# Loading both plain x tiles ahead of the first K row, and taking the last output columns as 512, 288 and 224

## The chip, the cores and the metric

The kernel runs on 1 core of one Trainium2 chip. The metric is the device time of one execution in microseconds; the profile gives a span that is some 1.5 us shorter. "Dense stream" below means the 30 matmuls of 512 columns that run back to back once the first weights are there.

## The reference, cut to what matters

```python
x = A_x                                             # 1 x 2048 x 1024, bf16
g = sigmoid((x * gate_w).sum(-1, keepdims=True))
a = linear_attention(x, wqkv, wo)                   # 32 heads of 32, phi(q), phi(k)
b = x + scatter_of_one_row(ffn(x[argmax(x @ w_r)])) # one routed token
return g * a + (1 - g) * b
```

The kernel first needs K and V for all tokens: x transposed, against the K and V columns of `wqkv`. It ends with one matrix product per 128 tokens against a merged matrix of attention state and `wo`, plus the mix with x.

## The kernel before: the parts concerned

The front. Two x tiles are loaded as they are and transposed on TensorE, the other tiles come by transposing fetches. The weights for K come as eight pieces of 256 KB, called K row 0 to 7 here.

```python
load_x(0, 1)
load_k(0)
load_x(1, 1)
for c in range(1, KC):
    load_k(c)
# ... V columns, transposing fetches, the rest of V, the Q weights
...
warm(N_WARM)                       # 6 matmuls of 512 columns on constants
...
unit_T(0)                          # 8 transposes, evicted by VectorE and ScalarE
warm(3, 128)
first_mm(0, 0, 1)                  # tile 0 x K row 0: 2 matmuls of 512
wps = ps_ffn.tile([P, 16], BF, tag="f")
pe.transpose(wps[:], wrg_rows[:], ident[0:16, 0:16])   # router and gate weights
dve.tensor_copy(wkv[:, :, 2 * D : 2 * D + 2], ...)
unit_T(1)
for c in range(1, KC):             # the dense stream
    first_mm(0, c, c + 1)
    if c < KC - 1:
        first_mm(1, c - 1, c)
```

The back, for the last of 16 token tiles: each group of columns is eight matmuls, one VectorE instruction from PSUM to SBUF, and its own store.

```python
cols = [(0, 512), (512, 512)] if t < NT - 1 else [(0, 512), (512, 384), (896, 128)]
for c0, cw in cols:
    ps = ps_work.tile([P, 512], F32, tag="w")
    for g in range(NG):
        pe.matmul(ps[:, 0:cw], lhsT=pq_all[...], rhs=m_sb[:, g, c0 : c0 + cw], ...)
    dve.scalar_tensor_tensor(ot[:, c0 : c0 + cw], ps[:, 0:cw], gate[:, t : t + 1], xg[...], ...)
    if t == NT - 1:
        nc.sync.dma_start(out=out2d[...], in_=ot[:, c0 : c0 + cw])
```

## Time and profile before

| | before |
|---|---|
| median of the first 3 runs | 248.74 us (248.62 to 249.12) |
| TensorE busy | 97% of the span |
| dense stream begins | 6.54 us, 0.04 after K row 1 lands |
| from the start of the first short column group to the last landing | 4.11 us |

The profile is of a run of 248.56 us. The prediction shows the page and the timelines. One more view is of use, the busy time of each engine by stretch (bounds, length, then busy time and number of instructions of each engine, granted clock, DMA share, GB/s), here of the kernel before:

```profile
0.00:3.00 3.00, 1.98 (x5) 0.73 (x6) 0.00 (x0) 1.10 (x1) 2.02 (x27) 1.00 0.32 80
3.00:6.50 3.50, 3.50 (x24) 1.88 (x23) 0.65 (x3) 0.77 (x2) 1.93 (x13) 1.00 0.99 334
```

From 3.0 to 6.5 us TensorE (first figure after the length) is shown busy in all 3.50 us, while the loads run at a DMA share of 0.99. Both look like the bound, and a busy TensorE does not say which: the warm-up matmuls on constants and the slow clock fill time that nobody needs. The clock column says nothing of that slow clock: its record begins when the full clock opens, at 6.09 us here, and the time before is shown as 1.00. The two rates are read from the steps of the 512-column matmuls, 0.427 us before and 0.216 after.

### The profile page before, as it was taken

To read this page: it belongs to the slowest core of one execution; us is meant where nothing else is said; L and a number is where in the kernel's file an instruction comes from. 1 tells how busy PE (TensorE), PEld (TensorE's weight loads), DVE (VectorE), ACT (ScalarE), POOL (GpSimd) and SP (SyncE) were. 2 spreads that over 40 slices of the span, in tenths; PEclk is the share of its full clock that TensorE was granted. 3 is DMA by queue.
4 is the path that set the end of the run, shared out by engine and by line. 5 is a ranking of instruction groups with operands and counts; after the bars stand their busy time and mean duration, and the time that the engine had idled before them with its cause. 6 is when DMAs were issued, how large, how long until landed. Compare 5 with 4: busy or idle time off the path is not lost.

```text
span 247.0 us, 4867 instructions
## 1 busy us (share of the span) xinstructions
PE 240.8 (97%) x1898; PEld 123.6 (50%) x1923; DVE 172.7 (70%) x264; ACT 127.6 (52%) x215; POOL 52.5 (21%) x100
## 2 busy tenths in 40 slices
PE   8999999999999999999999999999999999999994
PEld 3466756654554554554554555544443444444442
DVE  0053124379984989845989999996789999954342
ACT  3195343355566376545555555668887633333300
POOL 6000000400000100000003300101666689950000
PEclk9999999999999999999999999999999999999999
DMA  6999995499969993599699690000004754464122
GB/s 207 343 239 195 267 392 151 108 326 337 281 194 292 341 290 88 149 312 384 224 345 340 230 280 3 3 4 21 0 3 127 204 182 148 155 190 166 48 82 86
DMA packets 46311, 47.78 MB, mean 193 GB/s; under 512 B 16776, under 2 KB 35472, under 8 KB 46224
## 3 DMA queue, kind: packets, MB, share of 16 engines
q1 hardware_dynamic: 45648, 46.28, 61.5%
q0 software_dynamic: 608, 1.19, 1.7%
q8 instruction: 15, 0.25, 0.5%
q14 instruction: 8, 0.07, 0.1%
q10 hardware_dynamic: 32, 0.00, 0.0%
HBM read 39.33 MB, written 8.39 MB: 193 GB/s over the span
## 4 chain that ended last, share of the span: by engine, by line
PE 97%; issue 1%; DVE 0%; DVEq 0%
PE ps L83 88%; PE first L83 3%; PE kvacc L83 2%; PE warm_ps L83 1%; PE red L83 1%; PE dps L83 1%; PE pst L83 1%; PE pm L83 1%; DVE ot L83 0%; PE yps L83 0%; PE pt L83 0%; DVEq L739 0%; PE hps L83 0%; PE rps L83 0%; PE wps L83 0%
## 5 line engine op out<-in xcount | busy, mean ns | idle before, releaser
L83 PE MATMUL ps<-wkv,xT 128*128 128x352 bf16 (+2 forms) x600 | 106.1, 334 | 0.4
L83 PEld LDWEIGHTS <-xT 128*128 128x128 bf16 x640 | 62.1, 98 | 49.1 <-issue 0.3
L83 ACT ACTIVATE u<-ps 128x512 f32<-128x512 f32 x60 | 35.9, 598 | 46.3 <-PE ps L83 45.7
L83 PE MATMUL ps<-xT,wq 128*128 128x512 bf16 x245 | 57.3, 379 | 0.6 <-issue 0.2
L83 PE MATMUL ps<-m_sb,pq_all 128*128 128x512 bf16 (+2 forms) x259 | 55.4, 373 | 0.3
L83 ACT ACTIVATE e<-u 128x512 f32<-128x512 f32 x64 | 40.3, 630 | 2.0
L83 PEld LDWEIGHTS <-pq_all 128*128 128x128 bf16 x264 | 25.4, 98 | 30.2 <-issue 0.7
L641 POOL TENSOR_TENSOR pq_all<-pq_all,rb 128x512 bf16<-128x512 bf16 x32 | 36.4, 1171 | 12.1 <-DVE rb L83 11.5
L83 PEld LDWEIGHTS <-wq 128*128 128x128 bf16 x256 | 24.5, 98 | 28.2 <-issue 1.0
L83 DVE SCALAR_TENSOR_TENSOR gacc<-wt,hcol,gacc 128x1024 f32<-128x1024 bf16 x27 | 34.5, 1278 | 0.4
L83 DVE SCALAR_TENSOR_TENSOR ot<-ps,gate,xg 128x512 bf16<-128x512 f32 (+2 forms) x33 | 23.9, 738 | 14.3 <-PE ps L83 13.1
L83 DVE SCALAR_TENSOR_TENSOR gacc<-wt,xs_f,gacc 128x2048 f32<-128x2048 bf16 x14 | 32.8, 2345 | 0.2
L83 ACT ACTIVATE xg<-xt,omg 128x1024 f32<-128x1024 bf16 x16 | 18.2, 1147 | 26.8 <-DVE ot L83 25.8
L83 DVE SCALAR_TENSOR_TENSOR pq_all<-ps,e 128x512 bf16<-128x512 f32 x32 | 21.9, 687 | 11.3 <-ACT e L83 11.3
L83 DVE SCALAR_TENSOR_TENSOR pk<-ps,e 128x512 bf16<-128x512 f32 x28 | 19.0, 686 | 11.8 <-ACT e L83 11.6
L83 DVE STREAM_SHUFFLE rb<-rdp 128x512 f32<-128x512 f32 x32 | 22.8, 753 | 0.0
L83 ACT CAST vt<-ps 128x352 bf16<-128x352 f32 x32 | 14.4, 453 | 11.4 <-PE ps L83 11.1
L214 POOL MEMSET vt<- 128x22 bf16 x16 | 3.7, 432 | 75.7 <-PE kvacc L83 75.2
L83 ACT CAST vc<-ps 128x320 bf16<-128x320 f32 x16 | 6.5, 428 | 7.3 <-PE ps L83 7.3
L83 DVE COPY rg<-ps 128x2 f32<-128x2 f32 x16 | 2.5, 159 | 10.2 <-ACT vc L83 10.1
L355 POOL DMA_DIRECT2D xs<-in_A_x_dram x1 | 0.7, 711 | 39.3 <-DVE sig L83 39.3
L83 DVE SCALAR_TENSOR_TENSOR pk<-first,e 128x512 bf16<-128x512 f32 x4 | 2.8, 692 | 7.9 <-ACT e L83 7.9
(100 smaller groups left out, 94.9 us busy)
## 6 DMA issues: line engine op xcount, KB each, us to landing
wt<-in_B_w_down_dram SPq DMA_DIRECT2D x14, 512.0 KB, 4.9
wt<-in_B_w_gate_dram SPq DMA_DIRECT2D x8, 512.0 KB, 7.6
wt<-in_B_w_up_dram SPq DMA_DIRECT2D x8, 512.0 KB, 8.3
xt<-xp SPq DMA_DIRECT2D x16, 256.0 KB, 2.7
out_dram<-ot SPq DMA_DIRECT2D x15, 256.0 KB, 2.0
wt<-in_B_w_gate_dram SPq DMA_DIRECT2D x8, 384.0 KB, 7.6
wt<-in_B_w_up_dram SPq DMA_DIRECT2D x8, 384.0 KB, 7.2
wkv<-in_A_wqkv_dram SPq DMA_DIRECT2D x8, 256.0 KB, 4.4
```

What stands on the lines that cost most here:

```text
L83: inst = fn(*a, **k)
L214: nc.gpsimd.memset(vt_t[t][:, :, 32:33], 1.0)
L355: nc.gpsimd.dma_start(out=xs8[:], in_=x2d[bass.ds(idx_val, 1), :].rearrange("o (c p) -> (o c) p", p=P))
L641: nc.gpsimd.tensor_tensor(sl, sl, rb[:], op=ALU.mult)
```

## The change

Its intent: have the transposes of both tiles over before any K row is needed, so that these and the router transpose no longer stand between K row 0 and the dense stream; and balance the last two column groups, so that the last store isn't held up. The router transpose also takes its PSUM buffer from the pool of the tile transposes (`ps_t`, three buffers) in place of `ps_ffn`.

```diff
     load_x(0, 1)
-    load_k(0)
     load_x(1, 1)
-    for c in range(1, KC):
+    for c in range(KC):
         load_k(c)
...
     unit_T(0)
-    warm(3, 128)
-    first_mm(0, 0, 1)
-    wps = ps_ffn.tile([P, 16], BF, tag="f")
+    wps = ps_t.tile([P, 16], BF, tag="t")
     pe.transpose(wps[:], wrg_rows[:], ident[0:16, 0:16])
     dve.tensor_copy(wkv[:, :, 2 * D : 2 * D + 2], ...)
+    warm(2, 128)
     unit_T(1)
+    warm(4, 128)
+    first_mm(0, 0, 1)
...
-        cols = ... else [(0, 512), (512, 384), (896, 128)]
+        cols = ... else [(0, 512), (512, 288), (800, 224)]
```

More of the change, by code (lines that the diff above doesn't have):

```diff
@@ L696 @@
         ot = fin.tile([P, D], BF, tag="o3")
-        cols = [(0, 512), (512, 512)] if t < NT - 1 else [(0, 512), (512, 384), (896, 128)]
+        cols = [(0, 512), (512, 512)] if t < NT - 1 else [(0, 512), (512, 288), (800, 224)]
         for c0, cw in cols:
```

## The prediction

> **What bounds the kernel now.** I read the page first (busy shares, slices, chain of waits), then the timeline of TensorE over the first 26 us, then the landings of the loads that stand there, then the timeline of the last 5 us. The page:
>
> ```profile
> span 247.0 us, 4867 instructions
> PE 240.8 (97%) x1898; PEld 123.6 (50%) x1923; DVE 172.7 (70%) x264; ACT 127.6 (52%) x215; POOL 52.5 (21%) x100
> ...
> PE   8999999999999999999999999999999999999994
> ...
> PE 97%; issue 1%; DVE 0%; DVEq 0%
> ```
>
> TensorE is busy in all slices but the first and the last, and it is 97% of the chain that ended last. Matmul busy time includes pipeline drain, so I do not take it as distance from the peak. What matters is that there is no large hole: only the two ends, about 6.5 us at the front and 4 us at the back, can be changed by this diff, since it touches nothing between.
>
> The front, TensorE alone (start, length, name, idle time before in brackets):
>
> ```profile
> 1.02 2.72 PE L83 MATMUL warm_ps<-const-bfloat16-1.0 128*128 128x512 bf16 x6 [1.02 <-PEq L728]
> 3.72 1.03 PE L83 MATMUL pst<-ident,xnat 128*128 128x128 bf16 x8
> 4.55 0.53 PE L83 MATMUL warm_ps<-const-bfloat16-1.0 128*128 128x128 bf16 x3
> 4.87 1.06 PE L83 MATMUL first<-wkv,xT 128*128 128x512 bf16 x2
> 5.86 0.19 PE L83 MATMUL wps<-ident,wrg_rows 16*128 16x16 bf16 x1
> 5.98 0.65 PE L83 MATMUL pst<-ident,xnat 128*128 128x128 bf16 x8
> 6.54 6.63 PE L83 MATMUL first<-wkv,xT 128*128 128x512 bf16 x29
> 13.01 13.18 PE L83 MATMUL ps<-wkv,xT 128*128 128x322 bf16 x85
> ```
>
> The eight transposes of x tile 0 at 3.72 step by (4.55 - 3.72)/8 = 0.104 us, the eight of tile 1 at 5.98 by (6.54 - 5.98)/8 = 0.07 us, the last of them by about 0.055. From 6.54 to 13.01 there are 30 matmuls (one of 32 is missing from the records, two ran before): 0.216 us each, without a hole. The clock record says full speed from 6.1 us.
>
> The loads that stand there. First the plain x tiles (0 and 1), then K row 0 and K row 1 alone, then the V columns:
>
> ```profile
> DMA to landing us min/median/max: 2.7/3.2/3.8
> ```
> ```profile
> DMA to landing us min/median/max: 2.8/2.8/2.8
> ```
> ```profile
> DMA to landing us min/median/max: 4.1/4.1/4.1
> ```
> ```profile
> wkv<-in_A_wqkv_dram SPq DMA_DIRECT2D x1, 640.0 KB, 7.2
> ```
>
> x tile 0 is issued at 0.98 and lands at 3.7; K row 0 at 1.44, lands 4.3; x tile 1 at 1.90, lands 5.7; K row 1 at 2.39, lands 6.5. So the dense stream begins at 6.54 because K row 1 is there at 6.5; TensorE was itself done with the transposes at about 6.48. The V columns, issued at 5.71, land at 12.9, and their first matmul is at 13.01. A third gate stands at 20.68, where the first tile of the next group of x comes in by a transposing fetch:
>
> ```profile
> 20.68 5.31 PEld L83 LDWEIGHTS <-xT 128*128 128x128 bf16 x39 [0.18 <-DMA xT<-in_A_x_dram]
> ```
>
> The weight load came 0.18 us later than it could have, while the matmul behind it lost nothing. So at 6.5, 13.0 and 20.7 us TensorE and the loads arrive together, within 0.1 us. The front is as much bound by loads as by TensorE.
>
> The back (eviction of the 384 columns, of the 128 columns, the two stores):
>
> ```profile
> 242.94 0.62 DVE L83 SCALAR_TENSOR_TENSOR ot<-ps,gate,xg 128x384 bf16<-128x384 f32 x1 [0.49 <-PE ps L83]
> ```
> ```profile
> 243.47 0.34 DVE L83 SCALAR_TENSOR_TENSOR ot<-ps,gate,xg 128x128 bf16<-128x128 f32 x1
> ```
> ```profile
> 243.58 0.33 SPq L706 DMA_DIRECT2D out_dram<-ot  x1
> ```
> ```profile
> 244.01 0.38 SPq L706 DMA_DIRECT2D out_dram<-ot  x1
> ```
> ```profile
> out_dram<-ot SPq DMA_DIRECT2D x1, 128.0 KB, 1.7
> out_dram<-ot SPq DMA_DIRECT2D x1, 96.0 KB, 1.6
> out_dram<-ot SPq DMA_DIRECT2D x1, 32.0 KB, 1.5
> ```
>
> The last matmul ends at 243.35. The 128-column eviction ends at 243.81, but its store is issued only at 244.01: the store of the 384 columns holds the issuing engine from 243.58 to 243.92. The last store lands at 244.01 + 1.5 = 245.5, and the remaining 1.5 us to 247.0 is a closing sequence of semaphores that the change doesn't touch.
>
> **What the Trainium skill says.** "TensorE: Matmul & The Clock Gate", Part 1, says that the array runs at half rate until an activity window of about 3.4 us was busy, and that the window is free-running, so the moment varies from run to run. The trace agrees on the rates: about 0.107 us for 128 columns early, 0.216 us for 512 after 6.1. Part 4 of the same page says that transposes do not count as busy in the same way; nothing in this trace shows or denies it. "DMA: Bandwidth & Descriptors", Specifications, wants at least 512 B a piece for full rate, with read-modify-write below. At this size no penalty is seen: the store with 256 B rows took 1.5 us, that with 768 B rows 1.6. The same page, Anatomy of one DMA, puts a fixed cost of about 2 us on a transfer, mostly the receipt; here the fixed part is about 1.5, and it can't be split away.
>
> **The change part by part.**
>
> 1. The swap of loads. x tile 1 takes the second place, K row 0 the third; both are 256 KB with 2 KB pieces. I expect x tile 1 at about 4.3 (4.3 to 4.9) and K row 0 at about 5.7. K row 1 stays fourth, with the same bytes ahead, so it lands at 6.5 as before. The order of all later loads is unchanged, so their gates at 13.0 and 20.7 stay.
>
> 2. The order on TensorE. Before: 8 transposes, 3 short warm-up matmuls, 2 matmuls of K row 0 at the slow clock, the router weights' transpose, 8 transposes, 30 matmuls. After: 8 transposes, router transpose, 2 short ones, 8 transposes, 4 short ones, 2 matmuls of K row 0, 30 matmuls. Working forward from 4.55: the 16-row router transpose costs a change of shape on either side (before, it came 0.56 us after a matmul of 0.43, so 0.14 extra, and held the next one for 0.12): 4.55 + 0.14 + 0.12 = 4.81. Two short ones at 0.107: 5.02. x tile 1 is there. Eight transposes at 0.107: 5.88. In the built program their two PSUM banks are those of tile 0's first half and of the router transpose, both emptied by VectorE, the first at 4.79, so I see no wait of weight. Four short ones, two slow, and two fast once the clock opens at 6.1: about 6.2. Two matmuls of K row 0 at the full clock, 0.43: 6.63. Against 6.54 that is +0.09 us. What it wins is that these two no longer run at the slow clock (2 x 0.21 us); what it pays is 3 more short matmuls (0.2 to 0.3) and the transposes of tile 1, which now run wholly at half rate (0.86 against 0.56). If the clock opens earlier, TensorE waits for K row 1 at 6.5 and the front costs 0. So +0.05, between 0 and +0.1. It can hardly be a gain: K row 1, V columns and the transposing fetch hold it within 0.05 us of where it is.
>
> 3. The last columns. Eight matmuls of 384 and eight of 128 took 8 x 0.1625 + 8 x 0.0557 = 1.745 us. With the slope of these two, 288 costs 0.1224 and 224 costs 0.0957, and the sum is 1.745 again: the last matmul ends at the same 243.35. The 288-column eviction begins about 0.32 us before the old one and lasts about 0.51 (0.34 + 160 x 1.07 ns, from 384 in 0.62 and 128 in 0.34): it ends at about 243.14, and its store is issued from 243.16 to 243.50, out of the way. The 224-column eviction begins at about 243.39 (0.04 after the last matmul, as the 384 one did) and lasts 0.44: 243.83. Its store goes at once, 243.86 in place of 244.01, and lands in about 1.57 us (between 1.54 for 256 B and 1.63 for 768 B rows): 245.43 in place of 245.54. Gain 0.11 us.
>
> Sum: 248.74 + 0.05 - 0.11 = 248.68; I say 248.65.
>
> **The rivals.**
>
> Clock gate opens later. The short matmuls and the two of K row 0 kept the array busy before; in the new order the stretch from 3.7 to 5.9 is nearly all transposes. If these count little, the window that ended at 6.1 holds only about 1.4 us of counted work in place of about 2.0, the clock might stay low for one window more, to 9.5, and half of the 14 matmuls of that stretch would be lost: 3.0 us at half rate is 1.5 us lost, about 250.2. Against it: the author put six short matmuls around the transposes, and from 1.0 us there is nearly no idle time. I give it 0.15.
>
> The new order frees TensorE. If K row 1 came earlier than 6.5, the whole front could move by some tenths. For it: the x rows and K rows might not cost the memory the same. Against: the same bytes are ahead of it, and two more loads hold TensorE at 13.0 and 20.7. It would give 248.4 at best. I give it 0.1.
>
> The 448 B rows of the last store are slower than I take them, or the SBUF-side eviction of 224 columns eats the gain: then the back is 0, and the total 248.8.
>
> **Range and chances.** Three runs of before lie within 0.5 us, more than any part of this sum. The range 248.3 to 249.3 takes in the gain of the second rival and the small losses of the others; the late clock lies outside it. Two per cent is 5 us; no part of the front or the back is that long for this change to win or lose. Faster 0.01, same 0.98, slower 0.01.
>
> **What would show it.** Right: the 30 dense matmuls of first begin at 6.5 to 6.7, with x tile 1 landed before 5.0; the gate at 20.7 still there; the last store issued about 0.5 us after the last matmul's end in place of 0.66, and the distance from the 20.7 us gate to the last matmul unchanged. Wrong: matmuls of 512 columns at 0.43 us after 6.6 (the clock), K row 1 landing away from 6.5, or the fetch at 20.7 moved. A median below 248.2 or above 249.5 would mean that a step is missing.

## The result, and the profile after

| | before | after |
|---|---|---|
| median, 6 runs each | 248.81 us (248.62 to 249.52) | 248.93 us (248.66 to 249.12) |
| ratio | | 1.0001, 95% interval 0.9987 to 1.0014 |

The ratio is the mean time of the fast runs of one kernel over that of the other's of the same rounds (recomputed, it comes out with the profiled run left out), so it is not quite the ratio of the two medians. The interval is 0.35 us wide on either side, larger than any part of the predicted sum; from times alone nothing can be said but "the same". So the parts have to be read as distances inside the traces.

The front of TensorE in the changed kernel:

```profile
3.64 1.04 PE L83 MATMUL pst<-ident,xnat 128*128 128x128 bf16 x8
4.61 0.18 PE L83 MATMUL wps<-ident,wrg_rows 16*128 16x16 bf16 x1
4.72 0.29 PE L83 MATMUL warm_ps<-const-bfloat16-1.0 128*128 128x128 bf16 x2
4.85 0.61 PE L83 MATMUL pst<-ident,xnat 128*128 128x128 bf16 x8
5.29 0.39 PE L83 MATMUL warm_ps<-const-bfloat16-1.0 128*128 128x128 bf16 x4
6.12 7.35 PE L83 MATMUL first<-wkv,xT 128*128 128x512 bf16 x32 [0.44 <-DMA wkv<-in_A_wqkv_dram]
13.31 12.91 PE L83 MATMUL ps<-wkv,xT 128*128 128x322 bf16 x84
```

The transposes of tile 1 now come at 4.85 and everything before K row 0 is over at 5.5. With the two matmuls of K row 0, 0.43 us, TensorE could be ready for K row 1 at 5.95, where it was ready at 6.48 before; part of this is the clock, which opened at 4.65 here and at 6.09 before. Instead TensorE waits for K row 0 until 6.12. The merged line hides a second wait: two matmuls run at 6.12, the third begins at 6.84. The landings, x tiles first, then K row 0 (issued at 1.91), then K row 1 (issued at 2.40):

```profile
DMA to landing us min/median/max: 2.6/2.8/2.9
```
```profile
DMA to landing us min/median/max: 4.2/4.2/4.2
```
```profile
DMA to landing us min/median/max: 4.4/4.4/4.4
```

Both x tiles are there by 4.4, K row 0 at 6.1, K row 1 at 6.8. So the work was out of the way early, and the wait that had been hidden behind it now shows. The stretch view has TensorE busy 3.06 us where it was 3.50 before, at nearly the same DMA share (the earlier clock, at which a matmul is shorter, has a part in that too):

```profile
3.00:6.50 3.50, 3.06 (x27) 1.91 (x26) 1.02 (x3) 1.36 (x3) 1.95 (x13) 1.00 0.97 313
```

The back: the two short evictions, and the last two stores.

```profile
243.10 0.52 DVE L83 SCALAR_TENSOR_TENSOR ot<-ps,gate,xg 128x288 bf16<-128x288 f32 x1 [0.18 <-PE ps L83]
```
```profile
243.87 0.45 DVE L83 SCALAR_TENSOR_TENSOR ot<-ps,gate,xg 128x224 bf16<-128x224 f32 x1 [0.25 <-PE ps L83]
```
```profile
243.65 0.33 SPq L706 DMA_DIRECT2D out_dram<-ot  x1
```
```profile
244.35 0.33 SPq L706 DMA_DIRECT2D out_dram<-ot  x1
```
```profile
out_dram<-ot SPq DMA_DIRECT2D x1, 128.0 KB, 1.7
out_dram<-ot SPq DMA_DIRECT2D x1, 72.0 KB, 1.6
out_dram<-ot SPq DMA_DIRECT2D x1, 56.0 KB, 1.6
```

The 224-column eviction ends at 243.87 + 0.45 = 244.32 and its store goes at 244.35: the issuing engine, done with the other store at 243.98, is free. Before, 0.2 us lay between these two.

The spans split into four distances (us): the start of the dense stream; from there to the first matmul of the first short column group; from there to the last landing; from there to the end of the span.

| | dense stream | middle | back | close | span |
|---|---|---|---|---|---|
| before | 6.54 | 234.90 | 4.11 | 1.47 | 247.02 |
| after | 6.84 | 235.09 | 4.00 | 1.47 | 247.39 |

The back gained 0.11 (more exactly 4.108 against 3.995). The front and the middle lost 0.30 and 0.19. Are these two losses of the change, or chance? That is what the experiments are for.

**Theory A:** the front is set by the landing of the K rows in both kernels; the landing varies from run to run, and the change doesn't touch it. **Theory B:** the swap itself makes the K rows late. **Theory C:** TensorE's own front work and its clock set the start, and the loads only happen to be about as late.

### The profile page after: what moved, and what is told of

The parts are those of the page before. It is cut to its first block, busy times and chain, and to the rows that moved or that the text cites. A ratio compares the mean times of both kernels' runs of the same rounds, so it can differ in the third digit from the quotient of the medians.

```text
span 247.4 us, 4897 instructions
## 1 busy us (share of the span) xinstructions
PE 242.3 (98%) x1926; PEld 124.1 (50%) x1926; DVE 172.8 (70%) x264; ACT 127.7 (52%) x215; POOL 52.7 (21%) x100
## 4 chain that ended last, share of the span: by engine, by line
PE 96%; DMA 2%; SPq 1%; DVE 0%; issue 0%
PE ps L83 88%; PE first L83 3%; PE kvacc L83 2%; DMA wkv<-in_A_wqkv_dram 2%; PE red L83 1%; PE dps L83 1%; PE pm L83 1%; SPq L83 1%; PE yps L83 0%; DVE ot L83 0%; PE pt L83 0%; PE rps L83 0%; PE hps L83 0%; PE xs_ps L83 0%
## 5 line engine op out<-in xcount | busy, mean ns | idle before, releaser
L83 PE MATMUL ps<-xT,wq 128*128 128x512 bf16 x256 | 58.3, 379 | 0.0
```

The costliest lines, as they stand in the source:

```text
L83: inst = fn(*a, **k)
```

## The experiments

First both kernels again, unchanged, for the spread of their profiles, and each half of the change by itself.

**1. The kernel before, unchanged.**

> The kernel before, unchanged, for the spread of its profile. Theory A (the late K rows in the profile of the changed kernel are chance, one slow transfer): K row 1 lands anywhere between 6.4 and 6.9 us here too, and the moment of the full clock moves by more than 1 us between profiles of one kernel. Theory B (the swap makes the K rows late): K row 1 lands at 6.5 again, within 0.1. Ratio 1.000 either way.

Measured: 249.15 us (248.76 to 249.92), ratio 1.001 (0.9992 to 1.0028) against itself. Its profile:

```profile
5.73 0.18 PE L83 MATMUL wps<-ident,wrg_rows 16*128 16x16 bf16 x1
6.99 0.62 PE L83 MATMUL pst<-ident,xnat 128*128 128x128 bf16 x8 [1.09 <-DMA xnat<-in_A_x_dram]
7.65 6.64 PE L83 MATMUL first<-wkv,xT 128*128 128x512 bf16 x30
```
```profile
DMA to landing us min/median/max: 5.2/5.2/5.2
```

The landing line is that of K row 1: issued at 2.40, landed at 7.6, where the first profile of the same program had 6.5. The x tile before it was late too, at 6.95 in place of 5.68. A landing is recorded in 16 shares. 15 of the 16 shares of that tile had landed by 5.21; the last one, 1.7 us later, held up all. In the packet records one 2 KB packet, begun at 4.38, took 1.70 us, where 0.1 is usual. The records do not say to which share a packet belongs, so that this packet is the late piece is inferred. K row 1, behind the tile, had 15 shares by 6.02 and the last at 7.61, so the delay was handed on. A last share that came late also held K row 1 in experiments 3 (6.48, then 7.05) and 4 (6.12, then 7.15), in experiment 4 without any 2 KB packet over 0.6 us; why shares come late is open. The front of one and the same kernel moves by 1.1 us, about ten times the larger part of the predicted sum. The dense stream still begins 0.04 us after K row 1. In size the expectation missed twice: 7.6 is beyond its 6.9, and the full clock came at 5.54 in place of 6.09, a move of 0.55 us and not of more than 1 (experiment 5 has one of 1.9).

**2. The changed kernel, unchanged.**

> The changed kernel, unchanged. Theory A: K row 0 and K row 1 land away from the 6.1 and 6.8 us of its first profile, on average at 5.7 and 6.5; ratio 1.000. Theory B: 6.1 and 6.8 again, ratio 1.001. Both: from the start of the last 512-column group's successor to the last store's landing 4.0 us, where the kernel before has 4.1.

Measured: 248.82 us (248.73 to 249.36), ratio 1.0001 (0.9987 to 1.0016). K row 0 landed at 5.77, K row 1 at 6.65, the dense stream began at 6.69, the back took 4.00. K row 2 was late here (7.69) and cost a further 0.18 us inside the dense stream. So the landings of the changed kernel lie between the 6.49 and 7.61 of the kernel before, as theory A has it.

**3. The front alone**, which is the changed kernel with the old columns:

```diff
-        cols = ... else [(0, 512), (512, 288), (800, 224)]
+        cols = ... else [(0, 512), (512, 384), (896, 128)]
```

> The swap of loads and the new order on TensorE, with the old last columns. Theory A: ratio 1.000 to 1.0005, the start of the dense stream follows the landing of K row 1 by 0.05 us whatever that is. Theory B: ratio 1.001, K row 1 at 6.8.

Measured: 249.12 us, ratio 1.0011 (0.9997 to 1.0025). K row 1 at 7.05, the dense stream at 7.09; the middle 234.86, the back 4.11. The middle, with the same front, is the same as before, so the 0.19 us that the first profile of the change lost there isn't owed to the new front. Here the clock opened only at 6.69, just after the second matmul of K row 0 had begun at 6.66; at the full rate that one is over by about 6.9 (an estimate from the step of 0.216). So TensorE still waited for K row 1, but for less than 0.2 us.

**4. The last columns alone.**

```diff
-        cols = ... else [(0, 512), (512, 384), (896, 128)]
+        cols = ... else [(0, 512), (512, 288), (800, 224)]
```

> The last columns alone, with the old front. Both theories: the last store goes 0.15 us earlier after the last column group begins, and lands 0.11 us earlier; ratio 0.9995, not to be told from 1 by times alone. If the gain of the columns were nil, the distance from the first of the two short column groups to the last landing would be 4.1 as before, not 4.0.

Measured: 249.15 us, ratio 1.0006 (0.9992 to 1.002): the same within noise, and on the slower side for a change that should only gain. In the profiled run (249.19) the front explains it: K row 1 landed at 7.15. The distances are sharp: the last store is issued 2.43 us after the first short group begins (2.57 before), the last landing is at 3.99 (4.11 before). This distance repeats within 0.03 us over all kernels with equal columns and the same queues and loads; the times of one kernel scatter by over 1 us.

**5. Less to load.** The changed kernel without the load of tile 1, with a wrong result.

```diff
     load_x(0, 1)
-    load_x(1, 1)
+    xnat[1] = xnat[0]
```

> Wrong result on purpose: the changed kernel without the load of x tile 1, whose place the data of tile 0 takes; TensorE's work is the same. Theory A (the landing of the K rows sets the front, in both kernels): K row 1 lands some 0.6 us earlier than with tile 1 loaded, about 6.1, the dense stream begins 0.04 us after it or when TensorE is done with its own front work (5.9 to 6.6, by the clock), and the time falls by 0.3 to 0.7 us, ratio 0.997 to 0.999. Theory C (TensorE's own front work and the clock set it, the loads only happen to be as late): the time stays, ratio 1.000.

Measured: 248.70 us, ratio 0.9991 (0.9974 to 1.0007), the runs in two heaps, three at 248.37 to 248.45 and three at 248.96 to 249.25. The profile fell in the upper heap: K row 1 landed at 6.44, the clock opened at 6.93, and the dense stream began at 7.07, 0.63 us after K row 1. That one run speaks for theory C.

> A second look at the kernel without the load of x tile 1 (wrong result on purpose). Its first profile had a slow transfer (K row 1 at 6.4) and a late clock (6.9 us), so TensorE came 0.6 us after K row 1. If the clock opens before 6 us here, the dense stream begins at 5.9 to 6.2 or 0.04 us after K row 1; if it opens at 6.5 or later, TensorE's own front work sets the start, at 6.6 to 7.1.

Measured, in one look: 248.14 us, below every correct run told of in this document. The clock opened at 4.99, K row 1 landed at 5.72, and the front of TensorE reads:

```profile
5.02 0.61 PE L83 MATMUL pst<-ident,xnat 128*128 128x128 bf16 x8
5.47 0.40 PE L83 MATMUL warm_ps<-const-bfloat16-1.0 128*128 128x128 bf16 x4
5.70 7.07 PE L83 MATMUL first<-wkv,xT 128*128 128x512 bf16 x32
12.61 7.56 PE L83 MATMUL ps<-wkv,xT 128*128 128x322 bf16 x46
```

No wait is left; TensorE goes through its front work, and the dense stream begins at 5.70 + 2 x 0.216 = 6.13, 0.56 to 0.71 us earlier than in the two profiles of the change, whose clock was about as early. So TensorE's own work lets the first dense matmul begin at about 6.1 with an early clock and at 7.1 with a late one, and K row 1 of the kernel with the new front lands at 6.65 to 7.05. Theory A holds where the clock is early, which includes both profiles of the change (4.65 and 4.74 us); theory C holds where it is late, as in the first profile here. They are two limits less than 1 us apart, and which one binds changes from run to run. What bound the runs that were not profiled isn't shown.

**6. More to load.** The changed kernel with one load that nobody reads.

```diff
     load_x(1, 1)
+    spare = xin.tile([P, 1, D], BF, name="spare", bufs=1)
+    sp.dma_start(out=spare[:], in_=x_v[:, 0:1, :])
```

> The changed kernel with one more load of 256 KB, read by nobody, between x tile 1 and K row 0. Theory A (the K rows set the front): every K row lands some 0.65 us later, K row 1 at 7.1 to 7.7, the dense stream begins 0.04 us after it, and the time rises by 0.5 to 0.8 us: ratio 1.002 to 1.003. Theory C (TensorE's own front work sets it and the loads have slack): the dense stream comes later by less than half of that, ratio 1.000 to 1.001.

Measured: 249.26 us (248.87 to 251.41), ratio 1.0042 (1.0005 to 1.0079). In the profile K row 1 landed at 7.50 and the dense stream began at 7.55, 0.7 to 0.9 us later than in the two profiles of the change: the front moved with the loads, as theory A says, and TensorE's wait is for the K rows:

```profile
6.62 0.59 PE L83 MATMUL first<-wkv,xT 128*128 128x512 bf16 x2 [0.38 <-DMA wkv<-in_A_wqkv_dram]
7.55 6.63 PE L83 MATMUL first<-wkv,xT 128*128 128x512 bf16 x30 [0.33 <-DMA wkv<-in_A_wqkv_dram]
```

The time of that run, 249.06, rose by only 0.1 to 0.2, mainly since the close of the program took 1.03 us in place of 1.47. In all other traces the instructions that close the program have a pause of about 0.4 us after the last landing, and here they don't. One more DMA in the program changed that; why, no run tells. Two runs took 251.2 and 251.4 with a mean granted clock of 0.993 in place of 1.000: 0.7% of 247 us is 1.7 us, an estimate of what the slow clock cost them. The ratio contains these two, so it is no measure of the load. The other four runs have a mean of 249.12, 0.18 above the kernel before (248.94); with the 0.44 us of the close that is 0.62, within the 0.5 to 0.8 expected, if the close was short in all four, which one trace alone shows.

**7. Each half of the front by itself.** First the loads alone, with the old order on TensorE, as an edit of the kernel before:

```diff
     load_x(0, 1)
-    load_k(0)
     load_x(1, 1)
-    for c in range(1, KC):
+    for c in range(KC):
         load_k(c)
```

> Only the swap of the loads, with the old order on TensorE. Theory A: the old order needs K row 0 before the transposes of tile 1, so these come after K row 0 (about 5.8) and end at about 6.9: the dense stream begins 0.2 to 0.5 us after the landing of K row 1 in place of 0.04. Ratio 1.001 to 1.002, within noise. Theory B (the swap alone is what costs): it begins 0.04 us after K row 1, and K row 1 is late.

Measured: 250.19 us (249.22 to 251.32), ratio 1.0065 (1.0032 to 1.0098). The interval excludes 1, but two of the four runs, at 251.0 and 251.3, carry it. The profile, of a run of 249.35:

```profile
4.59 0.34 PE L83 MATMUL warm_ps<-const-bfloat16-1.0 128*128 128x128 bf16 x3
6.00 0.59 PE L83 MATMUL first<-wkv,xT 128*128 128x512 bf16 x2 [1.08 <-DMA wkv<-in_A_wqkv_dram]
6.53 0.18 PE L83 MATMUL wps<-ident,wrg_rows 16*128 16x16 bf16 x1
6.64 0.62 PE L83 MATMUL pst<-ident,xnat 128*128 128x128 bf16 x8
7.09 6.68 PE L83 MATMUL first<-wkv,xT 128*128 128x512 bf16 x30
```

TensorE stands for 1.08 us before K row 0, with tile 1 long there, then does router and tile 1, and is 0.48 us late for K row 1 (6.61).

> A second look at the swap of loads with the old order on TensorE, two of whose runs took 251 us and two 249.3. If the clock is behind that (TensorE idle for 1 us before K row 0), a 251 us run shows 512-column matmuls 0.43 us apart for 2 to 4 us after the dense stream begins, and the full clock after 8 us. If it is a slow transfer, it shows a K row landing 1 us or more after the one before it. A 249.3 us run shows neither.

Measured: 248.71 us. K row 0 landed early, at 5.31, and the dense stream began 0.04 us after K row 1. A 251 us run was not caught, so what they are remains open.

Then the order on TensorE alone, which is the changed kernel with the old loads (the same lines turned back) and the old columns:

> Only the new order on TensorE, with the old order of loads. Theory A: the transposes of tile 1 wait for x tile 1 (5.7 to 6.9), then come 8 transposes, 4 short matmuls and 2 of K row 0, about 1.1 us at the full clock: the dense stream begins 0.3 to 0.6 us after K row 1. Ratio 1.001 to 1.002. If the order on TensorE were worth something by itself, it would begin 0.04 us after K row 1 and the time would fall.

Measured: 249.27 us (249.13 to 249.59), ratio 1.0018 (1.0001 to 1.0036). The transposes of tile 1 waited for the tile until 6.00, and the dense stream began at 7.12, 0.21 us after K row 1 (6.91). The expectation of 0.3 to 0.6 was too high since K row 1 was late itself, but the sign is as expected. Measured as the lag of the dense stream behind K row 1, each half alone costs 0.2 to 0.5 us in its profile (the loads alone nothing when K row 0 is early); together they cost nothing in three profiles (0.04). So the diff's two halves belong together, as far as one or two profiles of each tell.

**8. The reason for the gain at the back.** The kernel before, with the last store issued by another queue:

```diff
-                nc.sync.dma_start(out=out2d[...], in_=ot[:, c0 : c0 + cw])
+                (nc.scalar if c0 + cw == D else nc.sync).dma_start(out=out2d[...], in_=ot[:, c0 : c0 + cw])
```

> The kernel before with one edit: the store of the last 128 columns is issued by ScalarE's queue. Theory A (the store of the 384 columns holds the issuing engine for 0.33 us, and the last store waits for that): it goes 0.03 to 0.1 us after the eviction's end, 243.85 in that profile's time in place of 244.01, so from the first of the short column groups to the last landing 3.95 us in place of 4.10. If the wait were the eviction itself, it would stay 4.10.

Measured: the eviction of the last 128 columns ends at 244.045, its store goes at 244.08:

```profile
244.08 0.38 ACTq L706 DMA_DIRECT2D out_dram<-ot  x1
```

That is 2.41 us after the short groups begin (2.57 before), so the wait was indeed for the issuing engine. The last landing was at 4.03 (4.11 before), short of the 3.95 expected: the store now took 1.62 us, begun 0.26 us after that of the 384 columns in place of 0.43. The time was 249.15 us (248.88 to 250.86), ratio 1.0033 (1.0003 to 1.0062). The interval excludes 1, but one run of 250.86 carries it, and the other three are 248.88 to 249.24. What that run was is open; its profile wasn't taken.

**9. A try at a faster version.** The changed kernel with tile 1 issued by ScalarE's queue and columns of 512, 336 and 176:

```diff
-        sp.dma_start(out=xt4[:, 0:n, :], ...)
+        (nc.scalar if t0 else sp).dma_start(out=xt4[:, 0:n, :], ...)
...
-        cols = ... else [(0, 512), (512, 288), (800, 224)]
+        cols = ... else [(0, 512), (512, 336), (848, 176)]
```

> Try at a faster version: the changed kernel with x tile 1 issued by ScalarE's queue, so that each K row is issued 0.46 us earlier, and with last columns of 512, 336 and 176. Front, theory A: K row 1 is issued at 1.9 in place of 2.4 and lands 0.1 to 0.4 us earlier than with one queue if no transfer straggles, the time falls by as much; if the transfers are bound by what lies ahead of them in bytes, K row 1 stays. Back: the last store is issued 2.37 us after the first of the short column groups begins (2.43 with 288 and 224), and the last landing is at 3.93 (4.00). Ratio 0.998 to 1.000.

Measured: 250.57 us (248.89 to 251.1), ratio 1.0045 (1.0014 to 1.0076), so slower by some 0.4%. The back did what was expected: last store 2.38 us after the short groups begin, last landing at 3.94. The front failed:

```profile
4.36 1.03 PE L83 MATMUL pst<-ident,xnat 128*128 128x128 bf16 x8 [0.62 <-DMA xnat<-in_A_x_dram]
```
```profile
6.92 2.70 PE L83 MATMUL first<-wkv,xT 128*128 128x512 bf16 x6
```

The second line is the stretch from 7.0 to 9.3 us: 6 matmuls of 512 columns. The changed kernel issued 11 from 6.84 on in about the same time:

```profile
6.84 2.54 PE L83 MATMUL first<-wkv,xT 128*128 128x512 bf16 x11
```

The two tiles, loaded side by side, both land at 4.1 to 4.3, so tile 0 comes 0.6 us later than when it goes first. K row 1, issued at 1.92 in place of 2.40, landed at 7.28, later than in both profiles of the change: the expected 0.1 to 0.4 us earlier was missed. TensorE stands idle until 4.36, and the full clock comes at 9.43 us. That is the first rival of the prediction, a late clock, seen in the one profile of this kernel. Four of the six runs took 250.5 or more; that the other three had the same cause isn't shown. It does not touch the change, none of whose 12 timed runs took over 249.36, but it shows that this front has little to spare.

No version beats both kernels clear of noise. The old front with the columns of this last try would be about 0.17 us ahead of the kernel before by its back (3.94 against 4.11), an estimate that no run of that pair confirms.

## Why the prediction was right

**The sum.** 248.65 was said, 248.93 and 248.82 were measured in two sets of runs, where the kernel before stood at 248.81 and 248.86. "Same" and the range hold. The error of 0.2 to 0.3 us is within the scatter of the loads. (Its own sum gives 248.68; for the last 0.03 it has no reason.) The number says little for the mechanism: the range is 1 us wide, each part is 0.11 us or less, and both ratios are 1.0001, with intervals that neither show nor exclude the predicted gain of 0.09. Of the prediction's own signs, x tile 1 before 5.0 and the store about 0.5 us after the last matmul (0.52) came true. In the first profile of the change others failed: the dense stream began at 6.84 and not at 6.5 to 6.7, K row 1 landed away from 6.5, and the wait at 20.7 was gone. That the total held all the same is in part luck.

**Part 1, the swap of loads.** x tile 1 was predicted at 4.3 to 4.9 and landed at 4.35, 4.36 and 4.56 in three profiles with the new front and loads. K row 0 was predicted at 5.7: 6.08, 5.77, 5.82. K row 1 at 6.5: 6.79, 6.65, 7.05; with the old order of loads and the same bytes ahead of it, it landed at 6.49, 7.61, 7.15, 6.22 and 6.91, and with the swap of the loads alone at 6.61 and 6.46. The means are 6.71 with the new order of loads and 6.88 with the old order: no difference that could be told from this spread, so theory B finds no support and "K row 1 stays" is not contradicted. What the prediction missed is the spread itself: it read 6.5 off one profile and treated it as a property of the kernel.

**Part 2, the order on TensorE.** The +0.05 was a mean of +0.09 (clock at 6.1) and 0 (earlier). In both profiles of the change the clock opened at 4.65 and 4.74, TensorE was ready for K row 0 at 5.5 to 5.7, and the lag behind K row 1 was 0.04 as before: the cost was 0, one of the two cases named. That the clock was early both times was luck: with a clock at 6.93 (experiment 5) TensorE's own work lasted until 7.07, later than K row 1 of either profile of the change. The prediction took the moment of the full clock from one trace, too; over all traces it was 3.80 to 6.93 us, and once 9.43. The three gates at 6.5, 13.0 and 20.7 were not fixed either. The first is real and moves with the loads; the other two were coincidences of one profile. At 13.0 TensorE came straight from the last K matmul (12.79 + 0.216 = 13.01). At 20.68 the idle time of 0.18 us before the weight load was misread: the seven loads just ahead of it have 0.12 each, so only 0.06 of it is a wait. In the first profile of the change the start came 0.30 us later, the V stage came 0.30 us later (13.31 against 13.01), and the wait at 20.7 was gone.

**Part 3, the columns.** The sum of matmul times stayed (last matmul 1.650 us after the first of the short groups against 1.691, with longer matmuls at the end), evictions of 0.52 and 0.45 us came where 0.51 and 0.44 were predicted, the store went 0.146 us earlier where 0.15 was predicted, and landed 0.11 us earlier, as predicted. The reason is shown by experiment 8.

**The rivals.** The late clock is seen in no run of this change, and in a neighbour of it. The freed TensorE did happen: in the first profile it could have been ready for K row 1 half a microsecond earlier than before (5.95 against 6.48, in part by the clock) and could not use it, as the argument against that rival said. One reason is that the swap only changes what is left to do after the third load: before, the eight transposes of tile 1 (0.46 to 0.55 us), now the two matmuls of K row 0 (0.43). The last rival, slow 448 B rows, did not happen: that store landed in 1.57 us, as estimated.

## What to carry to other kernels

When an engine and the loads it needs arrive together, taking work off the engine only uncovers the wait; test which of the two binds by taking one load away and by adding one. Before sizing a change of some tenths of a microsecond from landings in a profile, take a second profile of the same program: here one late share of sixteen moved the start by 1.1 us. Where times scatter more than the effect, measure the distance between two events of one trace that the effect lies between; it resolved 0.03 us where times resolved 0.35.

## What the Trainium skill lacked or had wrong

- "DMA: Bandwidth & Descriptors", Specifications, gives 512 B as the least piece for full rate. Stores to memory of 128 rows from this kernel landed, from issue, in 1.54 us with rows of 256 B, 1.57 with 448 B, 1.63 with 768 B and 1.72 with 1024 B: no step at 512 B. Most of that time is the same for all sizes, so the packet records say more: a packet of these stores took 18, 25, 36 and 46 ns (medians of 128), on a straight line with no step at 512 B either. The rate of larger transfers with such rows was not tested.
- The same page gives no figure for the spread of a landing from run to run. Fourth in its queue, the same 256 KB landed at 6.49 and 7.61 us in two profiles of one program, one packet of 2 KB taking 1.70 us in place of about 0.1 in the second.
- "TensorE: Matmul & The Clock Gate", Part 4, says that transposes do not count as busy in the same way. Part 1 of that page says that windows are 3.41 us long, and the traces agree: the full clock lasted 242.35 us in twelve of them and 238.93 in two, 71 and 70 such windows. Count back from the moment of the full clock, each matmul by its columns at the rate of the moment. In the first profile of experiment 5, the window that ended at 3.52 us held 2.50 us of plain matmuls and did not open the clock; the next one held 1.2 us of them and 1.7 us of transposes, and did. So transposes count, and for three quarters of their time at least if the same amount has to be reached (1.22 + 0.76 x 1.68 = 2.50). Over all 14 traces, windows with up to 2.50 us of both together did not open the clock and those from 2.51 on did. In experiment 9 the window that ended at 6.02 held 2.3, since TensorE had stood idle for tile 0; that fits its late clock. All this is argued from the traces, not tested by itself.
- No page has the 0.4 us pause in the instructions that close a program, which came after the last landing in all traces but that of experiment 6. The close took 1.47 to 1.62 us with it and 1.03 without.
